# Attention, gated MLP and experts in one kernel: a pooled product moved by one round, and held loads moved in their list

## The chip, the cores and the metric

The kernel runs on one core of a Trainium2 chip. The time is that of the device for one execution, in microseconds (us); of the runs shown the median counts. A core has a matrix engine (TensorE, PE in the profile, its weight loads PEld), three engines for elementwise work (VectorE or DVE, ScalarE or ACT, GpSimd or POOL), and SyncE (SP), which here issues the transfers. Every engine takes its instructions in its own order and waits on semaphores for the others.

## The reference

Attention has 2 batches and 8 heads, 576 tokens, 64 channels. Its output is the sum of two softmax attentions: one over queries, keys and values averaged over four tokens each, and a local one in which a token sees those at most three away. An MLP follows, then four experts weighted by `domain_probs`. Cut to what matters here:

```python
q_d, k_d, v_d = (t.reshape(B, H, Sd, 4, D).mean(axis=3) for t in (q, k, v))
out_up = np.repeat(sm_attn(q_d, k_d, v_d), 4, axis=2)          # pooled
scores = np.where(abs(pos[:, None] - pos[None, :]) < 4, scale * q @ k.T, -1e9)
out_local = softmax(scores) @ v                                  # local
x = out_up + out_local          # then moe: h = x @ w_in, g = h * relu6(h + 3) / 6, g @ w_out
                                # then moe2: sum over 4 experts of p * relu(x @ w1) @ w2
```

## The kernel before

**Stages.** The attention stage is the loop over rounds `t` from line 1116. A unit is one batch and one pair of heads, so there are NU = 8 units: 0 to 3 belong to batch 0, 4 to 7 to batch 1. In the trace the rounds begin about every 7 us; round 5 begins on TensorE at 42.34 us, round 6 at 51.00, round 7 at 59.30. From about 66 us the dense products of the MLP follow, later the experts.

**What a round does.** The order on TensorE, DVE, ScalarE and GpSimd is the order of the code. In round `t` TensorE runs four idle products on zeros (L605), the pooled scores of unit `t` (L728), the masks as a product (L652) and 72 small score products (L665); then four more idle products, the turning of unit `t-1`'s local weights (L712), the values of unit `t-2` (72 products L802 and 8 pooled ones L813), and the turning of unit `t-1`'s pooled weights (L782). ScalarE takes the pooled exponentials (L753, four), the local one (L689), the copies of the turned weights (L719, L720, L790), and the copy `pd` of a unit's pooled result (L821). DVE takes maxima and sums (L741, L682, L694) and adds the pooled result to the local one (L827).

**Result tiles.** Scores and turned weights take turns in the pool "pairs" with three buffers. `values` and `pool_last_v` take theirs from the pool "last", which has one buffer: whoever takes it next waits until the one before has been read.

**Pooled values of batch 1.** `pooled_v(1, 1)`, the last 16 pooled rows, is made by `pool_last_v`: one product (L485) on the rows of v's part 2 and a copy on ScalarE (L488). The other 128 rows are added on DVE by `add_four(0)` and `add_four(1)` (two L452 each) from the load "four", issued in two halves (L502). `values` of unit 4, in round 6, needs all of them.

**Weights.** `convert` puts pieces of the conversion of the weights between: on DVE L245, L255, L267, L276, L234, on ScalarE L221 and L229. From round 3 on a round ends with one or two such pieces.

**Loads.** The list `later` holds what is still to be loaded; `load_next` takes one entry at three places in a round (ahead of `less_max`, behind `normalise`, at the round's end) from round 2 on. An entry with a hold first writes one element of the target on DVE (L189), and the load waits for it. Loads without a hold, and parts of a load that the held element does not touch, go out as soon as their buffer is free. SP issues in one order, which the scheduler sets, and what waits there holds up what stands behind it. `load_k` and `load_q` with pair 3 bring keys and queries of units 6 and 7, whose pooled sums GpSimd makes in rounds 4 and 5. `last_v` brings v's part 1, second half, and part 2.

Of the kernel before, what the change touches and what calls it, by code (L numbers as in the profile page):

```python
# [31 lines left out]
NHP = H // 2  # L32
# [31 lines left out]
NU = B * NHP  # L64
# [61 lines left out]
def model(ctx: ExitStack, tc: tile.TileContext, qT, kT, v, dp, w_in, w_out, w1, w2, out):  # L126
# [15 lines left out]
    def banks(last=False):  # L142

        pool = psum["last"] if last and "last" in psum else psum["pair"]
        return pool.tile([P, 2, 512], F32, tag="pair", name="pair")
# [13 lines left out]
    def take(dtype=F32, order=("slots", "mlp1")):  # L159

        pool = next(n for n in order if unused.get(n))
        unused[pool] -= 1
        return pools[pool].tile([P, SLOT], dtype, tag="slot", name="slot"), pool
# [23 lines left out]
    def hold(part):  # L187

        nc.vector.memset(part[:1, :1], 0.0)  # L189

    def load_half(i, h):
        if h == 0:
            raw[i] = take(order=SHORT)
            loaded[0] = i + 1
        part = slice(h * WT, (h + 1) * WT)
        hold(raw[i][0][:, part])
        nc.sync.dma_start(out=raw[i][0].bitcast(I32)[:, part], in_=sources[i][:, part])
# [191 lines left out]
    def load_k(pair, at=0, n=2, held=False):  # L389

        b, hp = divmod(2 * pair + at, NHP)
        if pair not in k_slots:
            k_slots[pair], q_slots[pair] = take(), take()
        k = k_slots[pair][0][:, at * SK : (at + n) * SK].rearrange("p (u s) -> p u s", u=n)
        for edge in (slice(0, FACTOR - 1), slice(SK - FACTOR + 1, SK)):
            nc.gpsimd.memset(k[:, :, edge], 0.0)
        if held:
            hold(k[:, 0, FACTOR:])
        nc.sync.dma_start(out=k[:, :, FACTOR - 1 : FACTOR - 1 + S], in_=kT[b, :, hp : hp + n])

    def load_q(pair, at=0, n=2, held=False):

        b, hp = divmod(2 * pair + at, NHP)
        q = q_slots[pair][0][:, at * S : (at + n) * S]
        q = q.rearrange("p (u s c) -> p s u c", u=n, s=2)
        if held:
            hold(q_slots[pair][0])
        for s in range(2):
            nc.sync.dma_start(out=q[:, s], in_=qT[b, s, :, hp : hp + n, :])

    def load_qk(pair, at=0, n=2):
        load_k(pair, at, n)
        load_q(pair, at, n)

    def v_rows(b, p, p0, first, rows, j0, j1):
        src = v[b, first : first + rows]
        (row, _), (one, _) = src.ap
        nc.sync.dma_start(
            out=v_slots[b][p][0][p0 : p0 + rows, : NJ * DM].rearrange("p (j n) -> p j n", j=NJ)[
                :, j0:j1  # L420
            ],
            in_=bass.AP(src.tensor, src.offset, [[row, rows], [QB * row, j1 - j0], [one, DM]]),
        )

    def load_v(b, p, parts=(0, 1)):
        if 0 in parts:
            v_slots.setdefault(b, []).append(take())
        slot, o = v_slots[b][p][0], FACTOR - 1
        if b and p < 2:
            hold(slot[:, 2 * DM * parts[0] :])  # L430
        if p == 0:
            if 0 in parts:
                nc.vector.memset(slot[:o, :DM], 0.0)
                v_rows(b, p, o, 0, WR, 0, 1)
                v_rows(b, p, WP, WP - o, WP, 0, 1)
                v_rows(b, p, 0, QB - o, P, 1, 2)
            if 1 in parts:
                v_rows(b, p, 0, 4 * QB - o, P, 2, 4)
        elif p == 1:
            for n in parts:  # L440
                v_rows(b, p, 0, (8 + 4 * n) * QB - o, P, 2 * n, 2 * n + 2)
        else:
            at = 16 * QB - o
            nc.vector.memset(slot[QB:W, DM : 2 * DM], 0.0)
            v_rows(b, p, 0, at, WP if b else WR, 0, 1)
            if b:
                v_rows(b, p, WP, at + WP, LAST_ROWS - WP, 0, 1)
            v_rows(b, p, 0, at + QB, QB, 1, 2)
            v_rows(b, p, QB, at + 2 * QB, o, 1, 2)
# [4 lines left out]
    def pooled_v(b, kc):  # L454

        return v_slots[b][NP - 1][0][: KR[b][kc], (2 + kc) * DM : (3 + kc) * DM]
# [25 lines left out]
    def pool_last_v():  # L482

        to = banks(True)[: KR[1][1], 0, :]
        nc.tensor.matmul(  # L485
            to, last_fours, v_slots[1][NP - 1][0][:LAST_ROWS, :DM], start=True, stop=True
        )
        nc.scalar.activation(out=pooled_v(1, 1), in_=to, func=AF.Copy)  # L488
# [7 lines left out]
    def load_four(part):  # L496

        if part == 0:
            four_slots.append(take())
        to, cols = four(part)  # L500
        hold(to[:, 0])
        nc.sync.dma_start(  # L502
            out=to, in_=v[1].rearrange("(p f) d -> p f d", f=FACTOR)[: KR[1][0], :, cols]
        )

    def add_four(part):
        of, cols = four(part)
        add(nc.vector, of[:, :2], of[:, :2], of[:, 2:])
        add(nc.vector, pooled_v(1, 0)[:, cols], of[:, 0], of[:, 1])
        if part:  # L510
            give(four_slots.pop())
# [62 lines left out]
    def make_last_fours():  # L574
        nc.gpsimd.memset(last_fours, 1.0)
        for sign, at in ((1, -(FACTOR - 1)), (-1, 2 * (FACTOR - 1))):
            nc.gpsimd.affine_select(
                out=last_fours,
                in_=last_fours,
                pattern=[[-sign * FACTOR, KR[1][1]]],  # L580
                base=at,
                channel_multiplier=sign,
                compare_op=ALU.is_ge,
                fill=0.0,
            )
# [495 lines left out]
    def pieces(n, ps=None):  # L1081
        for _ in range(n):
            if early:
                first(*early.pop(0), ps)


    def last_v():
# [3 lines left out]
    later = [  # L1091
        lambda: load_half(0, 0),
        lambda: load_half(0, 1),
        lambda: load_v(1, 0, (0,)),
        lambda: load_v(1, 0, (1,)),
        lambda: load_v(1, 1, (0,)),
        last_v,
        lambda: load_k(NU // 2 - 1, held=True),
        lambda: load_q(NU // 2 - 1, held=True),
        lambda: load_four(0),  # L1100
        lambda: load_four(1),
        lambda: load_half(1, 0),
        lambda: load_half(1, 1),
        lambda: None,
        lambda: load_half(2, 0),
        lambda: None,
        lambda: load_half(2, 1),
# [2 lines left out]
    def load_next(t):  # L1110
        if t > 1 and later:
            later.pop(0)()
# [3 lines left out]
    for t in range(NU + 2):  # L1116
        if t == NU:
            psum.pop("last").release()
            psum["few"] = ctx.enter_context(
                tc.tile_pool(name="few", bufs=2, space=PSUM, side="right")  # L1120
            )
        if t < NU:
            n = units[t]
            if t == 0:
                n.masks(IDLE)
                n.scores()
                n.pooled_scores(0)
                n.less_max()
                units[1].sums()
                n.pooled_softmax()  # L1130
                n.normalise()
            else:
                n.pooled_scores(4)
                n.masks(0)
                n.scores()
                n.pooled_softmax()
                if t == 1:
                    units[0].pooled_normalise()
                    make_last_fours()
                    units[2].sums()  # L1140
                    load_qk(2)
                load_next(t)
                n.less_max()
        if t == NHP + 1:
            pool_last_v()
        if t == NHP + 2:
            add_four(1)
        if 2 < t < NU + 1:
            units[t - 3].low()
        if 0 < t < NU:  # L1150
            n.pooled_normalise()
            n.normalise()
            load_next(t)
        if 0 < t < NU - 2:
            units[t + 2].sums()
        if t == NU:
            pieces(1, banks()[:, 0, :TC])
        if t >= NU:
            units[t - 2].values()
        if t > NU:  # L1160
            pieces(1)
            units[t - 3].low()
            units[t - 2].low()
        if 1 <= t <= NU:
            units[t - 1].turn(0 if t in (1, NU) else 4)
        if 2 <= t < NU:
            units[t - 2].values()
        if t == 1:
            pool_v(8)
        if 1 <= t <= NU:  # L1170
            units[t - 1].pooled_turn()
        if t == NHP + 1:
            add_four(0)
        convert(3 if t >= NU else 2 if t == 3 else 1 if t > 3 else 0)
        load_next(t)
        if t >= NU:
            pieces(1)
# [219 lines left out]
```

## Time and profile before

| what | us |
|---|---|
| median of 3 runs (lowest, highest) | 653.11 (652.74, 654.41) |
| the profiled execution | 653.55 |
| its span, first to last instruction | 651.4 |
| TensorE busy in the span | 642.8 (99%) |
| DVE busy | 417.8 (64%) |
| ScalarE busy | 252.7 (39%) |
| GpSimd busy | 95.8 (15%) |

Busy time of TensorE is not TensorE at its peak: a matrix product also counts as busy when it runs at half clock, and the idle products on zeros count too. The profile tells the granted clock of a stretch as a share: 1.00 is 2.4 GHz, 0.50 is 1.2 GHz. In brackets behind a row of the timeline stands how long the engine was idle before it, and what ended that.

### The profile page before, as it was taken

Reading aid. Unit: us, or ns where it says so; the run is one execution under the profiler, and the core shown is the slowest. Engines: PE = TensorE matmul, PEld = TensorE weight load, DVE = VectorE, ACT = ScalarE, POOL = GpSimd, SP = SyncE. Lnnn points to the kernel's source line nnn. Section 1 sums busy time; section 2 is a strip of 40 time slices with the busy share of each in tenths; the row PEclk is TensorE's granted clock in tenths of the full one; section 3 lists DMA queues with packets and bytes.
Section 4 is the critical chain, followed back from the end, with each engine's and each line's share of the span. In section 5 each row is a group of like instructions: output and inputs, shape, how many; then the busy total and the mean of one; then the engine's idle time right before and its main releaser. Section 6 shows DMA issues by size and latency. Waiting matters only on the chain.

```text
span 651.4 us, 11939 instructions
## 1 busy us (share of the span) xinstructions
PE 642.8 (99%) x4909; PEld 581.5 (89%) x4909; DVE 417.8 (64%) x848; ACT 252.7 (39%) x590; POOL 95.8 (15%) x141
## 2 busy tenths in 40 slices
PE   7999999999999999999999999999999999999997
PEld 3556899999999999998898998998998998988986
DVE  6578799962596228595575665665665765765742
ACT  5566576542464235352232233233241341331310
POOL 4753100000000035200201201201201201201000
PEclk9988999999999999999999999999999999999999
DMA  8754424500330110300110110110110210300012
GB/s 260 243 175 148 187 84 138 186 1 1 130 130 0 65 65 1 130 2 1 65 65 0 66 65 0 65 65 2 64 65 1 87 45 0 130 1 1 2 49 97
DMA packets 13368, 46.97 MB, mean 72 GB/s; under 512 B 1385, under 2 KB 4457, under 8 KB 9602
## 3 DMA queue, kind: packets, MB, share of 16 engines
q1 hardware_dynamic: 13314, 46.21, 21.0%
q8 instruction: 38, 0.62, 0.4%
q14 instruction: 16, 0.13, 0.1%
HBM read 43.85 MB, written 2.36 MB: 71 GB/s over the span
## 4 chain that ended last, share of the span: by engine, by line
PE 95%; DMA 2%; DVE 1%; SPq 1%; ACT 0%; issue 0%; POOL 0%; ACTq 0%; POOLq 0%
PE bank L994 27%; PE bank L382 10%; PE bank L383 10%; PE bank L384 10%; PE bank L1273 10%; PE bank L1274 10%; PE bank L1275 10%; PE pair L802 2%; PE pair L605 2%; DMA slot<-in_qT_dram 1%; PE pair L813 1%; DMA slot<-in_v_dram 1%; PE pair L728 1%; PE pair L782 1%; PE pair L665 1%; PE pair L712 0%
## 5 line engine op out<-in xcount | busy, mean ns | idle before, releaser
L994 PEld LDWEIGHTS bank<-xop,slot 128*128 128x128 f32 x1344 | 180.0, 188 | 1.2
L994 PE MATMUL bank<-xop,slot 128*128 128x288 f32 x1344 | 180.8, 295 | 0.0
L1274 PE MATMUL bank<-slot,h 128*128 128x512 f32 x288 | 112.2, 390 | 0.0
L1273 PE MATMUL bank<-slot,h 128*128 128x512 f32 x288 | 112.1, 389 | 0.0
L1275 PE MATMUL bank<-slot,h 128*128 128x512 f32 x288 | 112.1, 389 | 0.0
L1281 DVE SCALAR_TENSOR_TENSOR slot<-bank,pr,slot 128x512 f32<-128x512 f32 x63 | 47.3, 750 | 80.7 <-PE bank L1275 80.7
L452 POOL TENSOR_TENSOR st<-slot 128x256 f32<-128x256 f32 x16 | 13.8, 862 | 462.0 <-DMA slot<-in_w_dram 232.0
L384 PE MATMUL bank<-h,slot 128*128 128x384 f32 x192 | 64.7, 337 | 0.0
L382 PE MATMUL bank<-h,slot 128*128 128x384 f32 x192 | 64.7, 337 | 0.0
L383 PE MATMUL bank<-h,slot 128*128 128x384 f32 x192 | 64.7, 337 | 0.0
L1275 PEld LDWEIGHTS bank<-slot,h 128*128 128x128 f32 x288 | 54.1, 188 | 11.4
L1273 PEld LDWEIGHTS bank<-slot,h 128*128 128x128 f32 x288 | 54.1, 188 | 10.7
L1274 PEld LDWEIGHTS bank<-slot,h 128*128 128x128 f32 x288 | 54.1, 188 | 10.6
L382 PE MATMUL bank<-x,slot 128*128 128x384 f32 x188 | 63.2, 336 | 0.0
L384 PE MATMUL bank<-x,slot 128*128 128x384 f32 x188 | 63.0, 335 | 0.0
L383 PE MATMUL bank<-x,slot 128*128 128x384 f32 x188 | 63.0, 335 | 0.0
L452 DVE TENSOR_TENSOR u<-bank,u 128x288 f32<-128x288 f32 x96 | 43.6, 454 | 20.4 <-PE bank L994 20.0
L1023 ACT ACTIVATE h<-c 128x288 fp32r<-128x288 f32 x64 | 27.7, 445 | 70.8 <-DVE c L452 70.8
L312 ACT ACTIVATE slot<-st 128x512 fp32r<-128x512 f32 x32 | 19.2, 624 | 63.0 <-POOL st L306 63.0
L883 DVE TENSOR_TENSOR h<-slot,h 128x384 fp32r<-128x384 f32 x48 | 27.0, 576 | 24.1 <-ACT h L882 24.0
L874 ACT ACTIVATE t<-bank,half__145 128x384 f32<-128x384 f32 x47 | 27.0, 580 | 38.7 <-PE bank L384 38.5
L875 DVE SCALAR_TENSOR_TENSOR slot<-t,bank 128x384 f32<-128x384 f32 x47 | 25.7, 551 | 24.3 <-ACT t L874 24.1
(121 smaller groups left out, 925.4 us busy)
## 6 DMA issues: line engine op xcount, KB each, us to landing
slot<-in_w_dram SPq DMA_DIRECT2D x16, 1024.0 KB, 4.9
slot<-in_w_out_dram SPq DMA_DIRECT2D x8, 1024.0 KB, 5.0
slot<-in_w_in_dram SPq DMA_DIRECT2D x5, 1024.0 KB, 5.9
slot<-in_v_dram SPq DMA_DIRECT2D x8, 512.0 KB, 5.5
slot<-in_w_in_dram SPq DMA_DIRECT2D x6, 512.0 KB, 4.4
out_dram<-slot SPq DMA_DIRECT2D x9, 256.0 KB, 2.0
slot<-in_kT_dram SPq DMA_DIRECT2D x3, 576.0 KB, 4.4
slot<-in_qT_dram SPq DMA_DIRECT2D x6, 288.0 KB, 5.0
```

The lines of the kernel that those rows point to most:

```text
L382: nc.tensor.matmul(ps, wh, xh, start=first, stop=False)
L383: nc.tensor.matmul(ps, wh, xl, start=False, stop=False)
L384: nc.tensor.matmul(ps, wl, xh, start=False, stop=last)
L452: eng.tensor_tensor(out=out, in0=a, in1=b, op=ALU.add)
L874: nc.scalar.activation(out=t, in_=ps, func=AF.Relu, bias=half_, scale=1.0 / (6.0 * UP))
L883: nc.vector.tensor_tensor(out=g[:, 1, :], in0=u, in1=r32(g[:, 0, :]), op=ALU.subtract)
L994: nc.tensor.matmul(ps, a[:, i, k], b[:, j, k], start=start and k == 0 and n == 0, stop=stop and k == 1 and n == 2, skip_group_check=True,)
L1023: nc.scalar.activation(out=self.h[:, 0, i, j], in_=of, func=AF.Relu)
L1273: nc.tensor.matmul(ps, hh, w[:, 0], start=(f == 0), stop=False)
L1274: nc.tensor.matmul(ps, hh, w[:, 1], start=False, stop=False)
L1275: nc.tensor.matmul(ps, hl, w[:, 0], start=False, stop=(f == NF - 1))
L1281: nc.vector.scalar_tensor_tensor(out=to, in0=ps, scalar=share, in1=to, op0=ALU.mult, op1=ALU.add)
```

## The change

The product `pool_last_v` is called in round 6 (`t == NHP + 2`) instead of round 5, between the scores and the pooled softmax, so that its copy stands ahead of that round's exponentials. In the list `later` an empty entry moves from the thirteenth place to the third, and the keys and queries of pair 3 come ahead of v's part 1 and `last_v`. Every load of v for batch 1, and "four", thereby comes at a later place of the rounds, "four" in round 5 instead of rounds 4 and 5.

```diff
--- before.py
+++ after.py
@@ -1091,17 +1091,17 @@
     later = [
         lambda: load_half(0, 0),
         lambda: load_half(0, 1),
+        lambda: None,
         lambda: load_v(1, 0, (0,)),
         lambda: load_v(1, 0, (1,)),
+        lambda: load_k(NU // 2 - 1, held=True),
+        lambda: load_q(NU // 2 - 1, held=True),
         lambda: load_v(1, 1, (0,)),
         last_v,
-        lambda: load_k(NU // 2 - 1, held=True),
-        lambda: load_q(NU // 2 - 1, held=True),
         lambda: load_four(0),
         lambda: load_four(1),
         lambda: load_half(1, 0),
         lambda: load_half(1, 1),
-        lambda: None,
         lambda: load_half(2, 0),
         lambda: None,
         lambda: load_half(2, 1),
@@ -1133,6 +1133,8 @@
                 n.pooled_scores(4)
                 n.masks(0)
                 n.scores()
+                if t == NHP + 2:
+                    pool_last_v()
                 n.pooled_softmax()
                 if t == 1:
                     units[0].pooled_normalise()
@@ -1141,8 +1143,6 @@
                     load_qk(2)
                 load_next(t)
                 n.less_max()
-        if t == NHP + 1:
-            pool_last_v()
         if t == NHP + 2:
             add_four(1)
         if 2 < t < NU + 1:
```

Two places show what this does to the order. The first is ScalarE at the end of round 5 and in round 6, before the change: L790 copies turned pooled weights, L229 converts weights, L753 and L689 are round 6's exponentials, L719 and L720 copy turned weights.

```order
L790 ACTIVATE aTd<-pair 128x2x144
L790 ACTIVATE aTd<-pair 16x2x144
L229 ACTIVATE slot<-slot 128x512 x2
L753 ACTIVATE exd,smd<-pair,nm 72x144 x4
L689 ACTIVATE ex_124<-ex_124 128x2x5x38
L719 ACTIVATE aT<-pair 128x384
```

And the same place of the changed kernel.

```order
L790 ACTIVATE aTd<-pair 128x2x144
L790 ACTIVATE aTd<-pair 16x2x144
L229 ACTIVATE slot<-slot 128x512 x2
L488 ACTIVATE slot<-pair 16x512
L753 ACTIVATE exd,smd<-pair,nm 72x144 x4
L689 ACTIVATE ex_124<-ex_124 128x2x5x38
```

The copy L488, which stood behind round 5's L689, has come between round 5's weight conversion and round 6's exponentials.

The second place is SP's queue in rounds 3 to 5, before the change. Here the buffers' numbers are kept: slot_630 is v's part 1, slot_720 its part 2, slot_784 and slot_785 are keys and queries of pair 3, slot_891 is "four", slot_972 the second block of `w_in`.

```order
L418 DMA slot_630<-in_v_dram 128x2x512 x2
L418 DMA slot_720<-in_v_dram 64x512
L418 DMA slot_720<-in_v_dram 3x512
L418 DMA slot_720<-in_v_dram 32x512
L418 DMA slot_720<-in_v_dram 3x512
L399 DMA slot_784<-in_kT_dram 128x2x576
L409 DMA slot_785<-in_qT_dram 128x2x288
L502 DMA slot_891<-in_v_dram 128x4x256 x2
L197 DMA slot_972<-in_w_in_dram 128x1024 x2
```

The same place of the changed kernel: slot_715 and slot_716 are keys and queries, slot_797 is v's part 1, slot_885 its part 2, slot_949 "four", slot_1058 the second block of `w_in`.

```order
L399 DMA slot_715<-in_kT_dram 128x2x576
L409 DMA slot_716<-in_qT_dram 128x2x288
L418 DMA slot_797<-in_v_dram 128x2x512
L418 DMA slot_885<-in_v_dram 64x512
L418 DMA slot_797<-in_v_dram 128x2x512
L418 DMA slot_885<-in_v_dram 3x512
L418 DMA slot_885<-in_v_dram 32x512
L418 DMA slot_885<-in_v_dram 3x512
L502 DMA slot_949<-in_v_dram 128x4x256 x2
L197 DMA slot_1058<-in_w_in_dram 128x1024 x2
```

Keys and queries now stand ahead of v, and five loads of v stand between them and "four".

## Rows read from the trace of the kernel before

**Rows 1.** The page, chain that ended last, shares of the span by engine

```profile
PE 95%; DMA 2%; DVE 1%; SPq 1%; ACT 0%; issue 0%; POOL 0%; ACTq 0%; POOLq 0%
```

**Rows 2.** Windows: stretch, length, busy per engine, granted clock, DMA share, GB/s

```profile
18.00:20.00 2.00, 2.00 (x23) 0.86 (x15) 0.00 (x0) 0.76 (x2) 1.64 (x4) 1.00 0.52 178
32.00:34.00 2.00, 1.65 (x20) 1.10 (x17) 0.30 (x3) 0.29 (x2) 2.00 (x3) 0.99 0.19 64
34.00:36.00 2.00, 2.00 (x9) 0.60 (x9) 1.90 (x4) 1.16 (x3) 1.84 (x4) 0.50 0.70 242
48.00:50.00 2.00, 1.63 (x76) 1.44 (x76) 0.66 (x3) 0.95 (x3) 1.91 (x3) 1.00 0.80 237
52.00:54.00 2.00, 2.00 (x12) 0.82 (x10) 1.93 (x5) 1.06 (x3) 0.65 (x1) 0.50 0.11 39
76.00:200.00 124.00, 124.00 (x712) 123.90 (x712) 98.39 (x181) 66.76 (x123) 0.00 (x0) 1.00 0.30 106
```

**Rows 3.** Chain of waits, 41.9 to 48.5 us: start, length, what

```profile
42.30 0.82 DVE xf L827 x2
43.12 1.67 DVE slot L255 x2
...
47.85 0.47 ACT slot L488
```

**Rows 4.** Timeline of TensorE, rounds 5 and 6: start, length, instruction, idle before

```profile
42.34 1.03 PE L605 MATMUL pair<-zeros 128*128 128x512 bf16 x4
...
45.00 1.02 PE L485 MATMUL pair<-slot,last_fours 67*16 67x512 f32 x2
...
48.37 1.35 PE L802 MATMUL pair<-aT,slot 38*64 38x32 f32 x72 [0.86 <-ACT slot L488]
...
51.00 1.88 PE L605 MATMUL pair<-zeros 128*128 128x512 bf16 x4
...
55.18 1.04 PE L605 MATMUL pair<-zeros 128*128 128x512 bf16 x4
...
56.67 1.35 PE L802 MATMUL pair<-aT,slot 38*64 38x32 f32 x72
```

**Rows 5.** Timeline of DVE, rounds 4 and 5

```profile
36.06 0.48 DVE L444 MEMSET slot<- 6x512 f32 x1 [0.17 <-issue]
...
50.94 0.82 DVE L827 TENSOR_TENSOR xf<-pair,pd 128x320 f32<-128x320 f32 x2 [2.18 <-ACT pd L821]
51.68 1.25 DVE L452 TENSOR_TENSOR slot<-slot 128x512 f32<-128x512 f32 x2
```

**Rows 6.** Timeline of ScalarE, rounds 5 to 7

```profile
54.08 1.18 ACT L229 ACTIVATE slot<-slot 128x512 fp32r<-128x512 f32 x2 [1.02 <-issue]
55.59 0.38 ACT L753 ACTIVATE exd<-pair,nm 72x144 f32<-72x144 f32 x1 [0.33 <-DVE nm L743]
...
61.30 1.23 ACT L221 ACTIVATE slot<-slot 128x512 f16<-128x512 bf16 x2
```

**Rows 7.** Timeline of SP, issues of transfers, rounds 4 and 5

```profile
35.93 1.83 SPq L418 DMA_DIRECT2D slot<-in_v_dram  x4
...
38.23 0.39 SPq L399 DMA_DIRECT2D slot<-in_kT_dram  x1
...
44.97 0.61 SPq L502 DMA_DIRECT2D slot<-in_v_dram  x1
```

**Rows 8.** Issues at 44.97, 45.84 and 59.44 us: count, size, us to landing

```profile
slot<-in_v_dram SPq DMA_DIRECT2D x1, 512.0 KB, 4.9
...
slot<-in_v_dram SPq DMA_DIRECT2D x1, 512.0 KB, 5.8
...
slot<-in_w_in_dram SPq DMA_DIRECT2D x1, 512.0 KB, 3.5
```

**Rows 9.** Timeline of TensorE's weight loads, round 8

```profile
68.29 0.44 PEld L802 LDWEIGHTS pair<-aT,slot 38*64 38x64 f32 x24 [0.25 <-ACT aTd L790]
```

**Rows 10.** Timeline of TensorE, round 1

```profile
16.39 1.93 PE L472 MATMUL pair<-slot,fours 38*16 38x512 f32 x20 [1.03 <-DMA slot<-in_v_dram]
```

## The prediction

> **What bounds the kernel now.** I read the page first. 95% of the chain that ended last is TensorE's own work [rows 1], so time is won or lost where TensorE waits or runs at its lower clock. The windows put both into the attention stage: from 76 to 200 us TensorE has no gap at all, while 48 to 50 us holds 1.63 us of matmul work, and the granted clock is 0.50, that is 1.2 GHz, in 34 to 36 and again in 52 to 54 us [rows 2]. The reader is to see that a stretch with a short wait comes some 3 us before each of the two.
>
> The chain of waits from 41.9 to 48.5 us names the second of these waits: in round 5 the copy L488 stands on ScalarE behind all exponentials and ends at 48.32 [rows 3]; the 72 value products L802 start at 48.37 after 0.86 us of idle time, and their releaser is that copy [rows 4]. They wait because their result tile comes from the pool with one buffer ("last"), which the pooled product L485 filled at 45.00 and which L488 must empty first.
>
> The low clock behind the wait has a price too. From the idle products at 51.00 to the next ones at 55.18 are 4.18 us; the same instructions in round 5 go from 42.34 to 45.00, 2.66 us [rows 4]. The difference is 1.52 us.
>
> **What round 5 loses.** L485 moves to round 6 and is paid once in either case. Without it, the idle products of round 5 start at 45.00 and L802 follows 1.49 us later (55.18 to 56.67 in round 6, where nothing waits), at 46.5 instead of 48.37. The pair that L802 writes was last read by L827, which ended at 43.12 [rows 3], so it is free. From L802 to the idle products of the next round are 2.63 us (48.37 to 51.00), from there at full clock 2.66 to the end of L665: 51.8. Then L485, about 1.0, and 1.49 to L802 in round 6: TensorE is ready for the values of unit 4 at 54.3. Before, they start at 56.67 [rows 4]. The 2.4 us between are the wait of 0.86 and the clock's 1.52, the most that this edit can give back.
>
> **What is late next.** L485 still fills the one-buffer pair ahead of L802, so in round 6 L802 waits for L488. On ScalarE L488 now stands ahead of the exponentials, but behind the two copies L229, which before ran from 54.08 to 55.26 [rows 6]. These wait for DVE's multiplications L276, and these stand on DVE behind add_four(0), L452 at 51.68 [rows 5], which reads the first half of the load "four". Before, that load was issued at 44.97 [rows 7], took 4.9 us [rows 8] and was there at 49.9, under cover of the wait for L827. The second edit moves it.
>
> In its new place five loads of last_v (the rest of v) stand ahead of it on SP, and one of them waits for DVE's L255, which ends at 44.79 [rows 3]. Before, five such loads held SP from 35.93 to the issue at 38.23, 2.3 us [rows 7]. So "four" is issued at about 44.8 + 2.3 = 47.1, 2.1 us later than before. Landing times of 512 KB in this stage are 3.5, 4.9 and 5.8 us [rows 8]: the weights land in 3.5, "four" itself in 4.9, its second half, with the first one in front, in 5.8. So it lands between 50.6 and 52.9; I take 4.9, since this is the same load with the same pieces, and get 52.0.
>
> DVE is ready for L452 earlier. The memset L444 (0.48 us [rows 5]) now stands ahead of round 5's pooled maximum, which makes that round's exponentials and pooled copy half a microsecond later than before; but TensorE's L813, which L827 waited for at 50.94 [rows 5], comes 1.9 us earlier. L827 then starts at about 49.7, held by ScalarE alone, and ends at 50.5. So DVE waits 1.5 us, to 52.0, for a load that cost nothing before. Queued behind it are L267, L276 and the next round's maxima on DVE, and through L276 also L229, L488 and the exponentials on ScalarE.
>
> From L452's start to L229's end are 55.26 - 51.68 = 3.58 us [rows 5, 6]: 55.6. L488 adds 0.5 [rows 3]: L802 starts at 56.15, against 56.67. With the landing at 52.9 it is 57.05, with 50.6 it is 54.75. So by the middle value 0.5 of the 2.4 us is left, and TensorE stands idle for 1.85 us, from 54.3 to 56.15, where the longest wait after 20 us was 0.86.
>
> Now the clock. After 0.86 us of waiting at 48.37 the clock was down at 52 to 54 us; 32 to 34 us, with 1.65 us of work, went the same way [rows 2, 4]. A wait of 1.85 us is worse, so I expect one stretch at 1.2 GHz in rounds 6 and 7, at the price of the one that goes, 1.52 us, paid in full because TensorE does not wait there before. The other bound is nothing. The Trainium skill (TensorE: Matmul & The Clock Gate, section on HAM oscillation) tells of the same in loops that wait for data: the wait throttles the work that follows. By that rule the sum is as I have it; without it the sum is rival A.
>
> **Other parts, at nothing.** The third keys go out about a microsecond before the 38.23 of now [rows 7], and GpSimd wants their sums only two rounds later. One half of the last queries no longer goes out in the first 20 us; the queries that TensorE waits for there were issued ahead of it. The memset L433 in round 3 delays DVE by the length of L444, under cover of the value products. The two halves of the second weight block follow L276 and are issued at about 55.2 and 56.4; with 3.5 us [rows 8] they are there at 59.9, before ScalarE's L221 at 61.30 reads them [rows 6]. If that cover goes, the exponentials of round 7 slip by what is missing.
>
> **The sum.** Against the profiled execution (span 651.4, 653.55 with the 2.15 us around it): -0.5 for L802's earlier start and +1.52 for the low clock that now lies behind it (the former one is contained in 56.67), together +1.0. The median of the runs is 653.11, 0.44 below the profiled one; I add the difference to the median: 654.1.
>
> **Rivals.**
> A: no low stretch follows the new wait: -0.5, or 652.6. For it: after a wait of 1.03 us before 16.39 [rows 10] the clock stayed at 1.00 in 18 to 20 us [rows 2]. Against it: both later ones went down.
> B, slower: "four" lands at 52.9 or later. L802 starts at 57.1, +0.4, and the exponentials of round 6, at 55.59 before [rows 6], start at the same time, 1.5 late. Most of that reaches the copy L790 of round 8, for which the values of unit 6 wait already, 0.25 us at 68.29 [rows 9], and the idle time on TensorE is 2.8 us. With one low stretch this is +1.9, with two +3.4: 655.0 to 656.5. It decides from a landing 5.8 us after issue on.
> C, faster: "four" lands in 3.5 us, as the weights did [rows 8], or at least by the time that DVE comes, 50.5. Then L229 ends at 54.1, L488 at 54.6, and L802 starts at 54.65 with hardly a wait and no low clock: -2.0, at most -2.4: 651.1 to 650.7. Against it: rows of 1 KB, and 0.6 MB issued just in front.
> On C the skill has a price: DMA: Bandwidth & Descriptors, section on the anatomy of one DMA, gives 2.0 us plus the bytes at 436 GB/s. An estimate from that page is 3.2 us for 512 KB, which would be C; the trace's 4.9 for this very load speaks against it.
>
> **How the numbers follow.** A measurement of this kernel tells about 0.3% (1.96 us) from no change: faster is below 651.15, slower above 655.07. The forecast has 0.42 (its own range 653.3 to 655.2), A 0.20, B 0.21, C 0.17. B lies above 655.07 nearly whole, and so does the forecast's upper end, 0.03; C lies below 651.15 in about three parts of four. Faster 0.13, same 0.64, slower 0.23. The range leaves out C's far end and the worst of B: 651.1 to 656.2.
>
> **What would show it.** Right: in round 5 no wait ahead of L802 and no low clock at 51 to 54 us; L452 at the end of round 5 idle for 1 to 2 us with the load of v as releaser; L802 of round 6 idle for about 2 us behind L488; the granted clock at 0.50 for a stretch between 56 and 64 us. Wrong: L452 with no idle time before it, L802 of round 6 starting before 55.3, or the clock at 1.00 from 54 to 66 us.

## The result and the profile after

| | runs | median us | lowest to highest |
|---|---|---|---|
| kernel before | 22 | 650.95 | 649.65 to 654.41 |
| changed kernel | 22 | 654.88 | 651.97 to 661.57 |

The ratio is 1.0057, with a 95% interval of 1.0041 to 1.0072: the change costs 3.7 us (2.7 to 4.7). That is slower by the bound of 0.3% named in the prediction (the 655.07 given there for it stands on a base of 653.11). The time lies within the range and 0.8 us from the 654.1 forecast; the change against the kernel before was forecast at +1.0, and "same" was the likeliest case. The median of before was 653.11 over three runs and is 650.95 over 22, so that a base 2.2 us too high and a step some 2.9 us too small (by the medians) nearly made up for each other: that the time came so near is luck.

The chain that ended last is TensorE's as before [rows 1], now with 94% by the page:

```profile
PE 94%; DMA 2%; DVE 1%; POOL 1%; issue 1%; SPq 1%; ACT 0%; POOLq 0%; ACTq 0%
```

The two profiled executions cannot be compared by their spans (651.4 and 651.3 us). Before's lost 3 us ahead of the place that the change touches, in part because its granted clock was down in 34 to 36 us [rows 2]: it was at round 4's value products (L802) only at 39.73, the changed kernel at 36.56. The new list has no part in this, since the kernel before, run again (e0 below), was there at 37.06. What the change touches is read from that instruction to the first product of the dense stage, the first L382. Of the kernel before, TensorE's timeline (start, length, instruction) has at these two points:

```profile
39.73 1.35 PE L802 MATMUL pair<-aT,slot 38*64 38x32 f32 x72
...
66.03 0.42 PE L382 MATMUL pair<-x,slot 128*128 128x384 f32 x1
```

The same view of the changed kernel, with the value products of rounds 4, 5, 6 and 7:

```profile
36.56 1.35 PE L802 MATMUL pair<-aT,slot 38*64 38x32 f32 x72
...
43.83 1.35 PE L802 MATMUL pair<-aT,slot 38*64 38x32 f32 x72
...
49.27 1.02 PE L485 MATMUL pair<-slot,last_fours 67*16 67x512 f32 x2
...
53.60 1.76 PE L802 MATMUL pair<-aT,slot 38*64 38x32 f32 x72 [1.83 <-ACT slot L488]
...
63.38 1.35 PE L802 MATMUL pair<-aT,slot 38*64 38x32 f32 x72
...
65.98 0.42 PE L382 MATMUL pair<-x,slot 128*128 128x384 f32 x1
```

From round 4's L802 to the first dense product are 26.30 us before and 29.42 after: +3.12, near the +3.7 of all runs. Round 5's wait of 0.86 [rows 4] is gone. Round 6's L802 comes 17.04 us after round 4's, where [rows 4] give 56.67 - 39.73 = 16.94: all that the move saves is used up by its wait of 1.83 us. The other 3.0 us lie behind it: from round 6's L802 to L382 are 12.38 us, before 66.03 - 56.67 = 9.36.

The windows of the changed kernel name what fills them (length; busy time of PE, PEld, DVE, ACT and POOL; granted clock; DMA share; GB/s):

```profile
52.00:54.00 2.00, 0.40 (x28) 0.40 (x28) 1.93 (x7) 2.00 (x6) 0.00 (x0) 1.00 0.29 39
54.00:56.00 2.00, 2.00 (x66) 1.55 (x58) 1.97 (x5) 2.00 (x9) 0.00 (x0) 0.59 0.77 279
56.00:58.00 2.00, 2.00 (x15) 1.43 (x14) 1.79 (x9) 0.30 (x2) 1.41 (x2) 0.50 0.60 195
58.00:60.00 2.00, 1.78 (x7) 0.80 (x8) 1.66 (x2) 2.00 (x5) 0.51 (x1) 0.50 0.73 238
60.00:62.00 2.00, 2.00 (x83) 1.27 (x80) 0.92 (x3) 0.58 (x2) 0.00 (x0) 0.71 0.11 45
```

52 to 54 us hold 0.40 us of matmul work. The clock is down from 54 to 61 us. What each stretch lacks of full clock is 0.41, 0.50, 0.50 and 0.29 of its two microseconds, together 3.4 us; at half clock that is 6.8 us at 1.2 GHz. It is twice what stood behind round 5's wait before: 3.4 us by the same sum over 50 to 56 us, from the granted clock of 0.50 in 52 to 54 us [rows 2] and of 0.76 and 0.89 in the windows beside it:

```profile
50.00:52.00 2.00, 2.00 (x17) 1.17 (x16) 1.06 (x3) 0.49 (x2) 1.84 (x5) 0.76 0.87 295
54.00:56.00 2.00, 2.00 (x80) 1.14 (x78) 1.93 (x6) 1.59 (x5) 0.00 (x0) 0.89 0.27 31
```

The way to the wait is the one that the prediction walked. By the order listed with the change six loads of v, not five, stand between the queries and "four". The first of them went out at 38.46. SP's timeline has the other five (L418), and "four" itself (L502) at 44.07, 7.51 us behind round 4's L802; before it was issued at 44.97 [rows 7], 5.24 us behind:

```profile
41.74 2.22 SPq L418 DMA_DIRECT2D slot<-in_v_dram  x5
...
44.07 0.89 SPq L502 DMA_DIRECT2D slot<-in_v_dram  x1
```

The list of DMA issues has its landing, the last number in us:

```profile
slot<-in_v_dram SPq DMA_DIRECT2D x1, 512.0 KB, 5.5
```

On DVE the sum L452 waits for it. On ScalarE L229 and then L488, the copy that round 6's L802 waits for, come behind it:

```profile
46.40 0.82 DVE L827 TENSOR_TENSOR xf<-pair,pd 128x320 f32<-128x320 f32 x2 [0.17 <-ACT pd L821]
...
49.59 1.16 DVE L452 TENSOR_TENSOR slot<-slot 128x512 f32<-128x512 f32 x2 [2.37 <-DMA slot<-in_v_dram]
...
51.12 1.29 DVE L276 TENSOR_TENSOR slot<-slot 128x512 f32<-128x512 f32 x2
```

```profile
51.90 1.18 ACT L229 ACTIVATE slot<-slot 128x512 fp32r<-128x512 f32 x2 [3.38 <-issue]
52.98 0.57 ACT L488 ACTIVATE slot<-pair 16x512 f32<-16x512 f32 x1
```

### The profile page after: what moved, and what is told of

It reads as the page before. It is cut to its first block, busy times and chain, and to the rows that moved or that the text cites. A ratio compares the mean times of both kernels' runs of the same rounds, so it can differ in the third digit from the quotient of the medians.

```text
span 651.3 us, 11926 instructions
## 1 busy us (share of the span) xinstructions
PE 641.7 (99%) x4895; PEld 582.3 (89%) x4909; DVE 417.3 (64%) x848; ACT 252.8 (39%) x590; POOL 95.2 (15%) x141
## 4 chain that ended last, share of the span: by engine, by line
PE 94%; DMA 2%; DVE 1%; POOL 1%; issue 1%; SPq 1%; ACT 0%; POOLq 0%; ACTq 0%
PE bank L994 27%; PE bank L382 10%; PE bank L383 10%; PE bank L384 10%; PE bank L1273 10%; PE bank L1275 10%; PE bank L1274 10%; PE pair L802 1%; DMA slot<-in_qT_dram 1%; PE pair L605 1%; PE pair L813 1%; DMA slot<-in_v_dram 1%; PE pair L782 1%; POOL slot L452 0%; PE pair L728 0%
## 5 line engine op out<-in xcount | busy, mean ns | idle before, releaser
L452 POOL TENSOR_TENSOR st<-slot 128x256 f32<-128x256 f32 x16 | 13.8, 862 | 462.5 <-DVE slot L317 205.2
L382 PE MATMUL bank<-h,slot 128*128 128x384 f32 x192 | 64.7, 337 | 0.0
L382 PE MATMUL bank<-x,slot 128*128 128x384 f32 x188 | 63.2, 336 | 0.0
L452 DVE TENSOR_TENSOR u<-bank,u 128x288 f32<-128x288 f32 x96 | 43.5, 454 | 20.6 <-PE bank L994 20.2
L875 DVE SCALAR_TENSOR_TENSOR slot<-t,bank 128x384 f32<-128x384 f32 x47 | 25.7, 551 | 24.4 <-ACT t L874 24.2
```

The costliest lines, as they stand in the source:

```text
L382: nc.tensor.matmul(ps, wh, xh, start=first, stop=False)
L452: eng.tensor_tensor(out=out, in0=a, in1=b, op=ALU.add)
```

## The experiments

Each was run twelve times, e2 four times, beside runs of the kernel before on the same chip, in three groups: e0, e1, e3 and e4, with a median of before of 651.60 (35 runs); e2, e5, e6 and e7, with 651.32 (29); e8 and e9, with 650.92 (23). The ratio is taken from the runs and is not that of the medians, which for e1 would be 1.0008, inside its interval. "Stage" is, in the profiled execution, round 4's L802 to round 6's L802, and from there to the first L382. "Low" is the time per run at 1.2 GHz as a mean over all runs, from each run's mean granted clock c as 2 (1 - c) 651 us. It counts the whole run, also stretches ahead of the change, such as 34 to 38 us in before's profile or 18 to 25 us in e4's. Over the 87 runs of the kernel before in the three groups it is 4.0 us.

| kernel | median us | ratio to before (95%) | low | stage |
|---|---|---|---|---|
| changed kernel | 654.88 | 1.0057 (1.0041 to 1.0072) | 8.9 | 17.04 + 12.38 |
| e0 before, again | 650.98 | 0.9985 (0.9964 to 1.0005) | 3.4 | 18.12 + 9.35 |
| e1 product moved, old list | 652.14 | 0.9986 (0.9964 to 1.0008) | 4.1 | 15.54 + 10.98 |
| e2 new list, product not moved | 660.73 | 1.0119 (1.0085 to 1.0154) | 15.6 | 26.10 + 9.35 |
| e3 empty entry put back | 652.76 | 1.0008 (0.9991 to 1.0026) | 3.8 | 15.54 + 9.73 |
| e4 first sum a round later | 650.68 | 0.9986 (0.9967 to 1.0006) | 3.0 | 14.95 + 10.79 |
| e5 multiplication ahead of the sum | 650.79 | 1.0002 (0.9979 to 1.0025) | 2.9 | 14.94 + 11.03 |
| e6 wait filled with idle products | 652.75 | 1.0017 (1.0000 to 1.0034) | 3.0 | 18.06 + 9.58 |
| e7 e4 and two more idle products | 650.54 | 0.9985 (0.9965 to 1.0004) | 2.6 | 14.94 + 10.78 |
| e8 e1 and GpSimd's sums earlier | 651.49 | 1.0001 (0.9981 to 1.0022) | 4.6 | 15.63 + 10.92 |
| e9 e8 and both sums in round 6 | 650.48 | 0.9984 (0.9964 to 1.0004) | 3.9 | 14.48 + 11.49 |

**e0, the kernel before unchanged** (no edit), to learn what is typical of it.

> The kernel before, unchanged, run as a kernel of its own so that each run's granted clock is listed beside its time. Theory 1 (the change makes DVE wait for the load four, that holds ScalarE's weight copies L229 and the pooled copy L488, TensorE stands idle ahead of the values of unit 4 in round 6, and low-clock stretches follow): the ratio is 1.000 within 0.002; the mean clock of a run goes in steps of about 0.0026 (3.4 us at half clock in 651), most runs show at most one such stretch (0.997 or more), and each costs 1.2 to 1.9 us. Rival (the low clock has no part in it): the times of the runs spread without following the clock.

The same program differs from itself by a ratio of 0.9985, so those of e1 to e9 with ratios of 0.998 to 1.001, all but e2 and e6, cannot be told from before. Its profiled execution, in windows as above, shows that the low clock comes and goes in it:

```profile
46.00:48.00 2.00, 2.00 (x69) 1.34 (x61) 0.06 (x2) 0.17 (x1) 2.00 (x3) 0.79 0.75 201
48.00:50.00 2.00, 2.00 (x13) 1.44 (x12) 1.49 (x4) 0.96 (x3) 1.84 (x4) 0.50 0.61 213
50.00:52.00 2.00, 2.00 (x11) 0.80 (x8) 1.97 (x4) 0.99 (x4) 0.18 (x1) 0.50 0.03 12
52.00:54.00 2.00, 2.00 (x78) 1.34 (x77) 1.49 (x5) 1.60 (x7) 0.00 (x0) 0.50 0.40 78
```

Here it lasts 6.8 us, in before's own profile 3.4 at this place, and four of the twelve runs had a mean clock of 1.000 and took 649.6 to 651.0 us.

**e1, the product alone** (before, with this edit):

```
-        if t == NHP + 1:
-            pool_last_v()
...
                 n.scores()
+                if t == NHP + 2:
+                    pool_last_v()
```

> The kernel before with the product L485 and its copy L488 moved to round 6 alone, the list of loads as before. Theory 1: L452 at the end of round 5 has no wait for four, the wait of 0.86 us ahead of round 5's L802 is gone, L802 of round 6 waits 0 to 0.9 us for L488; time between 648.5 and 651 against some 651 of before, ratio 0.997 to 1.000. Rival 2 (the move itself costs: the copy ahead of round 6's exponentials delays them and what follows): slower than before by 2 us or more, 653 to 655, with L802 of round 6 waiting for L488 by about 2 us as in the changed kernel.

Its DVE and TensorE timelines, and ScalarE's row behind them:

```profile
48.84 2.06 DVE L452 TENSOR_TENSOR slot<-slot 128x512 f32<-128x512 f32 x2
...
51.74 1.40 DVE L276 TENSOR_TENSOR slot<-slot 128x512 f32<-128x512 f32 x2
```

```profile
54.33 1.35 PE L802 MATMUL pair<-aT,slot 38*64 38x32 f32 x72 [0.99 <-ACT slot L488]
...
80.35 0.44 PE L382 MATMUL bank<-x,slot 128*128 128x384 f32 x1 [0.85 <-DVE slot L875]
```

```profile
52.62 1.18 ACT L229 ACTIVATE slot<-slot 128x512 fp32r<-128x512 f32 x2 [2.40 <-POOL slot L452]
```

With the old list nothing waits for "four". But L452 takes 2.06 us where it took 1.25 [rows 5], at a time when GpSimd runs its own sums (L452 too, for unit 7), and L229 ends 4.96 us behind L452's start instead of 3.58. So L802 waits 0.99, and the move alone brings nothing that can be measured; nor does it cost the 2 us of rival 2. Whether GpSimd's sums are the reason is taken up in e8.

**e2, the list alone** (before, with the new `later`; pool_last_v() stays in round 5):

```
         lambda: load_half(0, 1),
+        lambda: None,
         lambda: load_v(1, 0, (0,)),
         lambda: load_v(1, 0, (1,)),
+        lambda: load_k(NU // 2 - 1, held=True),
+        lambda: load_q(NU // 2 - 1, held=True),
         lambda: load_v(1, 1, (0,)),
         last_v,
-        lambda: load_k(NU // 2 - 1, held=True),
-        lambda: load_q(NU // 2 - 1, held=True),
...
         lambda: load_half(1, 1),
-        lambda: None,
```

> The kernel before with the changed list of loads alone; the product L485 and its copy stay in round 5. Theory 1: the two edits belong together: part 2 of v is now issued about when TensorE reaches L485 in round 5, so TensorE waits there 4 to 6 us for that load (5 us to landing), and one or two low-clock stretches follow; 656 to 660. Rival (the list costs nothing by itself and the moved product is what costs): 650 to 652, as before.

TensorE's timeline:

```profile
49.90 1.87 PE L485 MATMUL pair<-slot,last_fours 67*16 67x512 f32 x2 [5.79 <-DMA slot<-in_v_dram]
```

The last part of v, now two places further back, holds round 5's product for 5.79 us, and the granted clock is 0.50 to 0.68 in every window from 46 to 64 us. The two halves of the change belong together.

**e3, the empty entry back in its place** (on the changed kernel):

```
-        lambda: None,
         lambda: load_v(1, 0, (0,)),
...
         lambda: load_half(1, 1),
+        lambda: None,
```

> The changed kernel with the empty entry put back to the thirteenth place of the list, so that every held load comes one place earlier and four is issued at the end of round 4; keys and queries stay ahead of v's later parts, L485 and L488 stay in round 6. Theory 1: the wait of L452 for four falls from 2.4 us to under 0.7, that of L802 in round 6 from 1.8 to under 1; time 648.5 to 651.5. Rival 2 (the move costs) and rival 3 (the keys ahead of v cost): 653.5 to 655.5, as the changed kernel.

TensorE's and DVE's timelines:

```profile
53.10 1.36 PE L802 MATMUL pair<-aT,slot 38*64 38x32 f32 x72 [0.85 <-ACT slot L488]
...
78.59 0.45 PE L382 MATMUL bank<-x,slot 128*128 128x384 f32 x1 [1.59 <-DVE slot L875]
```

```profile
47.62 2.05 DVE L452 TENSOR_TENSOR slot<-slot 128x512 f32<-128x512 f32 x2
...
76.65 0.69 DVE L245 TENSOR_SCALAR slot<-slot 128x1024 int32<-128x1024 int32 x1 [2.06 <-DMA slot<-in_w_in_dram]
...
77.99 0.55 DVE L875 SCALAR_TENSOR_TENSOR slot<-t,bank 128x384 f32<-128x384 f32 x1
```

"Four" is there in time again, L452 is long as in e1, and there is no low clock in this execution. The stage is 4.1 us shorter than the changed kernel's, but the median gained only 2.1, and less than I expected. In this execution the first dense product starts at 62.83, and 16 us on TensorE waits 1.59 us for DVE's L875, which reads a result tile ("bank") and stands on DVE behind the conversion L245; that one had waited 2.06 us for a load of weights. e1 (0.85), e4 (0.36) and e8 (0.59) show the same wait of TensorE at 78 to 80 us. What it costs was not tested by a run of its own, and it is not what limits every gain: e5, e6, e7 and e9 do not show it.

**e4, the first sum one round later** (on the changed kernel):

```
-        if t == NHP + 1:
-            add_four(0)
...
         if t == NHP + 2:
+            add_four(0)
             add_four(1)
```

> The changed kernel with all loads where they are, but the additions add_four(0) (two L452) made in round 6 together with add_four(1), so that DVE does not wait for four in round 5. Theory 1: no wait of DVE behind L827 of round 5, L229 and L488 come 2 us earlier, L802 of round 6 waits under 0.6 us, its pooled products L813 may wait up to 0.5 for the additions; time 648.5 to 651.5. Rivals 2 and 3: unchanged, 653.5 to 655.5.

**e5, the multiplication ahead of the sum** (on the changed kernel):

```
+        convert(3 if t >= NU else 2 if t == 3 else 1 if t > 3 else 0)
         if t == NHP + 1:
             add_four(0)
-        convert(3 if t >= NU else 2 if t == 3 else 1 if t > 3 else 0)
```

> The changed kernel with two lines exchanged at the end of round 5: the weight conversion (L267, L276 on DVE) is issued ahead of add_four(0), so DVE still waits for four, but only the maxima of round 6 stand behind that wait and no longer L276, L229 and L488. Theory 1, the link over L276 and L229: DVE still waits 0.5 to 1.5 us ahead of L452, L229 is done 1.5 us or more earlier, L802 of round 6 waits for L488 by under 0.9 us instead of 1.83; time 649.5 to 652, mean low-clock time per run 3 to 5 us instead of 8.9. Rival (the wait of DVE reaches TensorE by another way, over the maxima and exponentials of round 6): 653.5 to 655.5.

TensorE's timeline of e4, then of e5:

```profile
54.82 1.36 PE L802 MATMUL pair<-aT,slot 38*64 38x32 f32 x72 [0.40 <-ACT slot L488]
...
56.67 0.86 PE L813 MATMUL pair<-aTd,slot 128*64 128x144 f32 x8 [0.49 <-DVE slot L452]
```

```profile
51.42 1.35 PE L802 MATMUL pair<-aT,slot 38*64 38x32 f32 x72
...
58.38 1.02 PE L605 MATMUL pair<-zeros 128*128 128x512 bf16 x3 [1.54 <-ACT aTd L790]
```

Both take the wait of DVE off the way to L488, in two ways, and both end 4 us below the changed kernel: this wait is the cause of the loss. In e5 DVE does not wait for "four" at all, against what I expected: L267 and L276 took so long beside GpSimd's sums (1.41 and 1.87 us) that the load was there first. In both, round 6's L802 comes 14.9 us after round 4's, 2.0 sooner than before, and 1.4 to 1.7 of that go again by L382 (10.79 and 11.03 against 9.36), in e4 mainly to the 0.49 above and another 0.49 for L790, in e5 to the 1.54 above. So they come back to before's time and not below it.

**e6, the wait filled** (on the changed kernel; the products are on zeros and change no value):

```
-            units[t - 1].turn(0 if t in (1, NU) else 4)
+            units[t - 1].turn(0 if t in (1, NU) else 12 if t == NHP + 2 else 4)
```

> The changed kernel with twelve idle products instead of four ahead of round 6's turning, 1.9 us of TensorE time that would else be spent waiting for L488. Theory 1 with the clock as the larger half of the cost: L802 of round 6 starts as late as in the changed kernel with 0 to 0.4 us of wait before it, the mean low-clock time per run falls from 8.9 us to 3 to 5, and the time from some 654.9 to 652 to 653.5. Rival 4 (the low clock does not come from this wait, or costs nothing): time 654 to 656, low-clock time unchanged.

The timelines of TensorE, DVE and ScalarE:

```profile
51.42 2.76 PE L605 MATMUL pair<-zeros 128*128 128x512 bf16 x11
...
54.63 1.35 PE L802 MATMUL pair<-aT,slot 38*64 38x32 f32 x72
```

```profile
48.64 1.26 DVE L452 TENSOR_TENSOR slot<-slot 128x512 f32<-128x512 f32 x2 [1.74 <-DMA slot<-in_v_dram]
```

```profile
52.13 0.57 ACT L488 ACTIVATE slot<-pair 16x512 f32<-16x512 f32 x1
```

DVE still waits for the load. Low clock falls from 8.9 to 3.0 us per run, in the profile the way from round 6's L802 to L382 from 12.38 to 9.58, and the loss from 3.9 to 1.4 us (each against before's median of its group; by the ratio from 3.7 to 1.1, 0.0 to 2.2). Products were added and the kernel became faster, so some 2.5 us of the loss, if not more, are the clock. This execution does not show the wait just filled: its clock was down in 46 to 50 us, TensorE was late for that reason, and L802 starts 1.9 us behind the end of L488, 18.06 us after round 4's instead of 17.04. Here the added products themselves cost time. What the other 1.4 us are, the late start or the products where they are not needed, is not shown.

**e7, e4's edit and two more idle products:**

```
-            units[t - 1].turn(0 if t in (1, NU) else 4)
+            units[t - 1].turn(0 if t in (1, NU) else 6 if t == NHP + 2 else 4)
```

> The version with the additions of four in round 6 (as e4_add_later), and six instead of four idle products ahead of round 6's turning, 0.48 us against its remaining wait of 0.40 us. Theory 1: low-clock time per run at or under 3 us, time 650.0 to 650.8, at or a little below both kernels. Rival: the two idle products are paid in full, 651 to 651.5.

With 650.54 against e4's 650.68 this tells nothing more: where the wait is 0.40 us, there is hardly any clock left to save.

**e8, GpSimd's sums ahead of its normalising** (on e1):

```
+        if t == NHP + 1:
+            units[t + 2].sums()
...
-        if 0 < t < NU - 2:
+        if 0 < t < NU - 2 and t != NHP + 1:
```

> The kernel with the moved product alone (as e1_move_only, list of loads as before), and GpSimd's sums for unit 7 taken ahead of round 5's normalising instead of behind it, so that they run before DVE's L452, L267 and L276. Theory 5 (in e1_move_only the gain of the moved product was lost because DVE's additions and conversions ran 1.4 us longer beside GpSimd's sums: 4.96 us from L452 to the end of L229 against 3.58 before): L452's first addition takes 0.7 us instead of 1.49, L229 ends 1 us or more earlier relative to L827, L802 of round 6 waits under 0.4 us instead of 0.99; time 649.5 to 651. Rival: the lengths stay (GpSimd is not the reason), 651 to 652.5; or GpSimd's normalising, now later, holds the turning L712 of round 6: a wait there, 651 to 653.

GpSimd's and DVE's timelines:

```profile
42.54 5.39 POOL L452 TENSOR_TENSOR slot<-slot 128x288 f32<-128x288 f32 x8 [2.48 <-DMA slot<-in_kT_dram]
47.89 1.32 POOL L769 TENSOR_TENSOR exd<-exd,recd 72x576 f32<-72x576 f32 x1
49.18 1.00 POOL L698 TENSOR_TENSOR ex<-ex,rec 128x380 f32<-128x380 f32 x1
```

```profile
46.94 1.27 DVE L452 TENSOR_TENSOR slot<-slot 128x512 f32<-128x512 f32 x2
48.14 1.37 DVE L267 TENSOR_SCALAR slot<-slot 128x1024 uint16<-128x1024 uint16 x1
49.54 1.80 DVE L276 TENSOR_TENSOR slot<-slot 128x512 f32<-128x512 f32 x2
```

L452 is back at 1.27, but not for the reason expected: GpSimd's sums still ran beside it, to 47.93. L267 and L276 now run beside L769 and L698 and are long, and so are these two. The gain that I expected is missing; L802 waits 1.09 for L488. The slowing moved and did not go.

**e9, e8 with e4's edit:**

```
-        if t == NHP + 1:
-            add_four(0)
...
         if t == NHP + 2:
+            add_four(0)
             add_four(1)
```

> As e8_sums_earlier, and the additions add_four(0) in round 6 beside add_four(1), so that nothing stands between L827 and the conversion on DVE in round 5. Theories 1 and 5: no wait of L802 in round 5 or 6 over 0.3 us, low-clock time per run at most 3 us; 649 to 650.5, below both kernels by 0 to 0.3%. Rival (what is won here is given back behind the attention stage, where the dense products wait for their weights): a wait of L382 near 78 to 81 us of 0.5 us or more, and 650.5 to 651.5.

L802 waits nowhere, the lowest median of all is 650.48, and its ratio of 0.9984 is that of e0. Low clock is 3.9 us per run, above the 3 expected; in the profile it follows a wait of 0.45 us of L813 for DVE's sums. The rival's wait of L382 did not come. No version here can be said to beat the kernel before; all but e2 beat the changed one.

## Why the prediction was right in its mechanism and too small in its size

- **Round 5:** forecast no wait ahead of its L802 and no low clock behind it. Shown: none.
- **The issue of "four":** forecast 2.3 us of SP from the first of five loads to it; it was 44.07 - 41.74 = 2.33. Forecast 2.1 us later than before; it was 7.51 - 5.24 = 2.27.
- **Its landing:** 4.9 us taken from the same load, 5.5 measured. It lies between the bounds of 3.5 and 5.8, nearer to rival B's. The estimate of 3.2 us that the prediction took from the Trainium skill (DMA: Bandwidth & Descriptors, Anatomy of one DMA) is further off than the row was. The page gives its figures for transfers on GpSimd's path, and SP issued this one.
- **DVE's wait at L452:** forecast 1 to 2, "1.5" by the middle value; it was 2.37, by the landing and because L827 ended earlier against the issue.
- **TensorE's wait:** forecast 1.85, measured 1.83, and this nearness is luck. Counted from round 4's L802, both its ends came 0.6 us later than forecast. TensorE was ready at 15.21 us (forecast 54.3 - 39.73 = 14.57), because round 5's L802 came 7.27 us after round 4's instead of 6.8. L802 started at 17.04 (forecast 56.15 - 39.73 = 16.42), because of the landing. So what the move gave back ahead of the wait was 1.7 and not 2.4 us, and the start, forecast 0.5 earlier than before, was 0.1 later.
- **The clock: this is the step that failed.** The prediction put it at "one stretch at 1.2 GHz in rounds 6 and 7, at the price of the one that goes, 1.52 us". It was 6.8 us at the low clock, and the way from round 6's L802 to the dense stage grew by 3.02. The 1.52 came from one execution behind a wait of 0.86 and stood for what follows one of 1.83. With the two terms as measured the prediction's sum is 0.10 + 3.02 = 3.1 where it had 1.0, against +3.7 in the medians. e6, which puts products where TensorE would wait and loses most of the low clock by it, shows that the clock is what grew, and e4 and e5, which take the wait away, that nothing else in the change costs as much.
- **What was refunded:** the low clock of the execution that was read was taken for every run's. That execution had two stretches, in 34 to 38 and 50 to 56 us. Over e0's runs the kernel before spends 3.4 us at the low clock (4.0 over the 87 beside the experiments), against 8.9 for the changed one.
- **Rivals:** A (no low clock) fell with the windows. C (a landing in time) did not come from the transfer, but e4 and e5 built its condition. Its 651.1 to 650.7 looks like what they measured, 650.68 and 650.79, but it stood for a gain of 2.0 to 2.4 us on a base of 653.11. By the ratio they gained 0.9 and lost 0.1 against before, neither clear of noise, and TensorE waited further on. B was nearest in size, 1.9 with one stretch and 3.4 with two; its condition, a landing 5.8 us after issue, was nearly met. Its path over the exponentials of round 6 to round 8 was not seen: round 8's L802 comes 2.3 us behind the first L382 in both kernels.
- **Parts at nothing:** the second weight block and the memsets showed no wait. GpSimd wanted the keys and queries of pair 3 sooner than the prediction has it: it waited 0.62 us for the queries, as it had waited 0.69 for the keys before, and TensorE did not wait for either. e2 shows that the list alone is not free: 9.4 us above its group's before, if the product stays in round 5 (7.7 by the ratio).

## What to carry to other kernels

A wait of TensorE in a stage of small products is to be priced with the clock that may follow it, as a mean over many runs and not by the stretch that one profile shows: with waits of 0.74 to 0.86 us the kernel before spent 3.4 to 4.0 us per run at the low clock, with one of 1.83 the changed kernel 8.9. A single execution can go either way. When a chain of engines is shortened, follow the transfers that had time under the old wait (here "four") and the engines that now meet (here DVE and GpSimd) before counting the gain. Before a median of three is taken as the base, see whether the clock of each run is the same.

## What the runs showed of the hardware that was not expected

- **The same program runs with 0 to 7 us of low clock.** Four of e0's runs at a mean clock of 1.000 took 649.6 to 651.0 us, four at 0.995 to 0.996 652.1 to 653.1; the changed kernel's went from 0.997 (652.0 to 652.6) to 0.986 (661.6). But a little low clock need not cost time: e0's four runs at 0.997 took 649.7 to 651.2, no more than those at 1.000, and of the 87 runs of the kernel before the 18 at 1.000 have a median of 651.34, the 22 at 0.997 one of 650.96 and the 15 at 0.995 one of 653.37.
- **A wait of one length was followed by quite different stretches of low clock.** In the profiled executions 0.86 us (before) were followed by 3.4 us of it, 0.74 (e0) by 6.8, 0.99 (e1) by 3.4, and 0.85 (e3) and 1.09 (e8) by none and 3.4; the 1.83 of the changed kernel by 6.8. e5's wait of 1.54 at 58.38, ahead of idle products, was followed by none, and e9's of 0.45 by 3.4. The Trainium skill (TensorE: Matmul & The Clock Gate, HAM oscillation) has a wait throttle the work behind it; the traces agree that it can, and e3 and e5 show that it need not. In e6, without that wait, TensorE still ran at 1.2 GHz for part of 46 to 50 us, ahead of round 6.
- **Work on DVE beside GpSimd's is slower in most of these cases, and so is GpSimd's.** L452's two sums took 1.25 to 1.27 us in before and e8, 2.05 and 2.06 in e3 and e1; L267 0.41 and 1.37; GpSimd's L769 1.14 in the changed kernel and 1.32 in e8. In e9 the pair L276 took 2.75 instead of 1.29:

```profile
47.81 0.42 DVE L267 TENSOR_SCALAR slot<-slot 128x1024 uint16<-128x1024 uint16 x1
48.27 2.75 DVE L276 TENSOR_TENSOR slot<-slot 128x512 f32<-128x512 f32 x2
```

The Trainium skill (SBUF — State Buffer, Who interferes with whom) has DVE and GpSimd take turns at a pair of ports that they share, where a DVE instruction reads two tensors from SBUF, and for some with one as well, of which it names tensor_scalar. The longer rows agree. But in the kernel before GpSimd ran beside L452 too, for 0.97 us of the 1.25 that it took at 51.68 [rows 5], and in e8 for 0.99 of 1.27; the two sums of round 6, beside which GpSimd stood idle, took 1.14. Before's GpSimd timeline has

```profile
49.98 2.67 POOL L452 TENSOR_TENSOR slot<-slot 128x288 f32<-128x288 f32 x4
```

What decides which of the two is slowed, and by how much, was not settled.
